# First mixture of a three-stage kernel: up products 512 columns wide, a result room for each kind of tile, four PSUM banks for transposes

## The chip, the cores and the metric

The kernel runs on one core of a Trainium2 chip. The metric is the device time of one execution in microseconds (us); three executions are timed and their median counts. The profile is one more execution, taken by the hardware profiler.

The engines are named as in the profile: PE is the matrix engine (PEld its weight loads, which overlap the products), DVE the vector engine, ACT the scalar engine, POOL the GpSimd engine, and SP the engine that issues most of the DMA transfers.

## The reference: attention, then two mixtures of experts

The rows of an attention output (4 batches of 576 tokens, 8 heads of 64) become x, 2304 rows of 512. The first mixture sends each row that passes a skip test to one of 8 experts, the second sends every row through all of 4 experts. The change is in the first:

```python
    do_compute = skip_score > 0
    xc = x[do_compute]
    e_idx = np.argmax(xc @ w_gate, axis=1)
    for e in range(E):                              # E = 8
        mask = e_idx == e
        h = np.maximum(xc[mask] @ w1[e], 0.0)       # w1[e] is 512 x 1024: the up product
        y[mask] = gate_w[mask, None] * (h @ w2[e])  # w2[e] is 1024 x 512: the down product
    out[do_compute] = xc + y
```

How many rows an expert gets is known only when the kernel runs.

## The kernel before

The program has three stages. Attention ends at about 230 us of the span; it leaves x in a DRAM buffer `XN`, and the rows that an expert will work on, each with its row number and gate weight behind it, in a DRAM buffer `XS` that has one region for each expert. The first mixture (`m1`) runs from about 235 to 410 us, and the second (`m2`) from there to the end.

`m1` goes through the experts in order. An expert's rows come in tiles of 128. Every expert has a **first tile** (the call of `m1_tile` with `y="y"`). Whether it has **further tiles** is tested on the chip by a branch on the count of rows (`more`, line 803, nested up to six deep, a loop behind it for the rest). The program holds the code of all of them; a tile that isn't needed is jumped over.

All products are made of three, to keep single precision with a fast data type: a tensor is cut into a high part and a low part (`xh`, `xl`), and high by high, high by low and low by high are added up in one PSUM bank. What `m1_tile` does for a tile of 128 rows:

- The up product, in two halves (`hf`) of 512 of the 1024 columns. Each half is one PSUM bank `hp`, filled as two quarters of 256 columns, each quarter by 12 products of 128x256 (line 710): four slices of the 512 deep sum by three. ACT takes the finished half out as `h`, with the ReLU (line 714).
- `h` is transposed on PE by four 128x128 products into a bank `tp` (`turned`, line 692), and cut into parts from there: ACT writes the high part `hi` (line 684), DVE the low part `lo` (line 685). The first half is transposed after the first quarter of the second half; the second half after the first four products of the down product (`n == self.YN`).
- `mid` transposes the rows of the next tile (`xg`, or `xi` for a further tile) in the same way, just before the down product or within it.
- The down product, 24 products of 128x512 into one bank `yp` (line 729).
- `m1_out`: DVE computes `ys` from `yp` and the rows (line 737), and POOL scatters it to `XN` by row number, with an indirect DMA (line 738). For a further tile this comes right behind the tile. For the first tile it is put off until the expert's further tiles are done (`out()` at the end of the loop over experts), so DVE does it as the next expert begins.

The `tp` tiles share a pool of two PSUM banks in turn (`ps_t`), so the third transposition of a tile goes into the bank of the first, and needs that bank read out by ACT and DVE. The `ys` tiles share two rooms in turn, in the order of the program text, in which the jumped-over tiles count.

Around the products, the weights are loaded by SP in tiles `r` of 512 KB (line 653; eight for an expert: four of `w1`, four of `w2`) and cut into a high part by ACT (line 661, `w1h`, `w2h`) and a low part by DVE (line 662, `w1l`, `w2l`). `sp` places these cuts by hand in the order of the first tile: two of this expert's `w2` tiles at its start, two more after the first half of the up product, and the next expert's four `w1` tiles after `n == 4` of the down product. On ACT and DVE the work stands in one queue in that order. In the trace experts 0 to 3 start at 237.4, 252.5, 266.3 and 280.5 us (expert 3 has one further tile, at 294.8), expert 4 at 309.8 with three further tiles, and experts 5 to 7 at 365.1, 383.3 and 397.1: 8 first tiles and 4 further ones.

Of the kernel before, what the change touches and what calls it, by code (L numbers as in the profile page):

```python
# [6 lines left out]
F32 = mybir.dt.float32  # L7
# [4 lines left out]
AF = mybir.ActivationFunctionType  # L12
ALU = mybir.AluOpType
AX = mybir.AxisListType
PSUM = bass.MemoryType.PSUM
# [37 lines left out]
class Kernel:  # L53
# [9 lines left out]
    XP = 2  # L63
    XB = 4
    YL = 5, 0
    YB = 2
    YN = 4
    LF = 99
    OT = 1
# [578 lines left out]
    def w_raw(self, w, i, e, c, pool=None):  # L648

        cols = slice(c * 256, (c + 1) * 256)  # L650
        r = pool.tile([128, 1024], F32, tag="raw", name=f"r{i + 1}") if pool else self.raw(1024, f"r{i + 1}")
        r = r.rearrange("p (k f) -> p k f", k=2 if i else 4)
        self.nc.sync.dma_start(r, (w[e, cols, :] if i else w[e, :, cols]).rearrange("(k p) f -> p k f", p=128))
        return r

    def w_split(self, pool, slot, i, raw, engines):

        hi, lo = (pool.tile([128, 1024], F32R, tag=f"w{x}{slot}", name=f"w{i + 1}{x}").rearrange(
            "p (k f) -> p k f", k=2 if i else 4) for x in "hl")
        h, l = engines  # L660
        (h.copy if h is self.nc.scalar else h.tensor_copy)(hi, raw)
        l.tensor_tensor(lo, raw, hi.bitcast(F32), ALU.subtract)
        return hi, lo
# [34 lines left out]
    def m1_tile(self, x, ws, sp=lambda n: None, mid=lambda: None, y="yi", late=0):  # L698

        nc, wk = self.nc, self.wk  # L700
        xg, xh, xl = x
        hs, hT = [], []
        sp(2)
        for hf in range(2):
            hp = self.ps_h.tile([128, 2, 256], F32, tag="h", name="hp")
            for c in range(2):
                w1h, w1l = ws[2 * hf + c]
                for i, (x, wx, k) in enumerate([(xh, wx, k) for k in range(4) for wx in (w1h, w1l)]
                                               + [(xl, w1h, k) for k in range(4)]):
                    nc.tensor.matmul(hp[:, c], lhsT=x[:, k], rhs=wx[:, k], start=(i == 0), stop=(i == 11))  # L710
                if hf and not c:
                    hT.append(self.parts(self.turned(hs[0]), "h"))
            h = wk.tile([128, 512], F32, tag="h", name="h")
            nc.scalar.activation(h, hp.rearrange("p a b -> p (a b)"), AF.Relu)
            hs.append(h)
            if not hf:
                sp(2)
        if not late:
            r = mid()
        yp = self.ps_y.tile([128, 512], F32, tag=y, name="yp")  # L720
        n = 0
        for hf in range(2):
            for x, c in [(x, c) for c in range(4) for x in range(2)] + [(2, c) for c in range(4)]:
                if late and n == late:
                    r = mid()
                if n == self.YN:
                    hT.append(self.parts(self.turned(hs[1]), "h"))
                    sp(4)
                nc.tensor.matmul(yp, lhsT=hT[hf][x // 2][:, c], rhs=ws[4 + 2 * hf + c // 2][x % 2][:, c % 2],  # L729
                                 start=(n == 0), stop=(n == 23))  # L730
                n += 1
        return r, lambda: self.m1_out(xg, yp)

    def m1_out(self, xg, yp):
        nc = self.nc
        ys = self.wk.tile([128, 512], F32, tag="y", bufs=self.YB, name="ys")
        nc.vector.scalar_tensor_tensor(ys, yp, xg[:, DM + 1:RW], xg[:, 0:DM], ALU.mult, ALU.add)  # L737
        nc.gpsimd.indirect_dma_start(out=self.XN, out_offset=bass.IndirectOffsetOnAxis(  # L738
            ap=xg[:, DM:DM + 1].bitcast(I32), axis=0), in_=ys, in_offset=None, bounds_check=N - 1, oob_is_err=False)
# [12 lines left out]
    def sp(self, n, upto):  # L752

        nc = self.nc
        en = dict(A=nc.scalar, V=nc.vector, P=nc.gpsimd)
        for _ in range(n):
            m = self.done1
            if m >= min(upto, len(self.plan)):
                return

            j = m // 2 % 6
            self.w.append([])
            self.w[-1] += self.w_split(self.wp[0 if j < 3 else 1], f"{j}{m % 2}", self.plan[m][1], self.raw1[m],
                                       [en[c] for c in self.SPE[m % 8]])
            self.done1 += 1
            self.fetch()
# [352 lines left out]
    def build(self):  # L1119
        tc, nc = self.tc, self.nc  # L1120

        def opener(st):
            return lambda name, bufs, **kw: st.enter_context(tc.tile_pool(name=name, bufs=bufs, **kw))

        with contextlib.ExitStack() as top:
            first = contextlib.ExitStack()
            top.enter_context(tc.manual_schedule() if self.MAN else contextlib.nullcontext())
            en = opener(top)
            cp, dr = en("cp", 1), en("dr", 1, space=DRAM)
            self.XS = dr.tile([E1 * N, RW], F32, name="XS")  # L1130
            self.XN = dr.tile([N, DM], F32, name="XN")
            self.ws = opener(first)("ws", self.RB)
            with contextlib.ExitStack() as st:
                en = opener(st)
                early = contextlib.ExitStack()
                self.qk, self.ep, kp = (opener(early)(x, i, side="right") for x, i in (("qk", 2), ("ep", self.EB), ("kp", 1)))
                ac = en("ac", 1)
                self.consts(cp, ac)
                self.attention_consts(ac, kp)
                self.xp = en("xp", 2)  # L1140
                self.hl, self.et, self.sm, self.sm2 = en("hl", self.HB), en("et", self.TB), en("sm", 4), en("sm2", 2)
                self.ps_s = en("ps_s", self.SB, space=PSUM)
                self.ps_t = en("ps_t", 2 if self.OT else 1, space=PSUM)
                self.ps_o = self.ps_t if self.OT else en("ps_o", 1, space=PSUM)

                def scored():

                    early.close()
                    self.ws3 = [opener(top)("wd", self.R3[0], side="right")]
                    self.wp = [opener(first)("wa", 1, side="right")]  # L1150
                    self.room += self.R3[0]

                self.attention(scored)
            with contextlib.ExitStack() as st:
                en = opener(st)
                self.wp.append(en("wb", 1))
                self.ws3.append(en("we", self.R3[1]))
                self.room += self.R3[1]
                self.wk, self.wx = en("wk", 2), en("wx", 2)
                self.ps_h, self.ps_t, self.ps_y = (en(x, i, space=PSUM) for x, i in (("ps_h", 2), ("ps_t", 2), ("ps_y", 1)))  # L1160
                raws = self.m1()
            first.close()
            en = opener(top)
            self.su, self.wu, self.wk2, self.xp = en("su", 2), en("wu", 2), en("wk2", 1), en("x2", 1)
            self.ps_u, self.ps_y = en("ps_u", self.PU, space=PSUM), en("ps_y2", 8 - self.PU, space=PSUM)
            self.m2(raws)
# [52 lines left out]
```

## Time and profile before

| | |
|---|---|
| Median of three executions | 1197.8 us (1197.21 to 1198.63) |
| The profiled execution | 1193.83 us, its span 1192.2 us |
| PE busy in the span | 1108.0 us, 93% |
| DVE, POOL, ACT busy | 767.6, 577.6, 505.9 us (64%, 48%, 42%) |
| First mixture, 235.5 to 409.7 us | 174.2 us, PE busy 160.3, DVE 102.8, ACT 92.4 |
| Mean granted clock of PE | 0.966 over the span, 0.98 in the first mixture |

The span runs from the first to the last instruction; the execution's own time is 1.6 us longer. PE counts as busy while a product is in it, and products overlap, so that a busy PE may still be slower than it could be. The granted clock is 1.00 at 2.4 GHz and 0.50 at 1.2 GHz.

### The profile page before, as it was taken

How to read it: one execution, taken by the hardware profiler on the slowest of the kernel's cores; microseconds unless marked ns; L12 is line 12 of the kernel's file. 1: busy time of each engine (PE TensorE's matmuls, PEld its weight loads, DVE VectorE, ACT ScalarE, POOL GpSimd, SP SyncE). 2: the span in 40 equal slices, each digit the busy share in tenths (PEclk: the TensorE clock that was granted, in tenths of full speed). 3: DMA queues.
4: the chain of work that ended last, by engine and by line, in shares of the span. 5: the costliest groups of instructions: out<-in, count | busy, mean ns of one | idle time of the engine just before them, and what ended most of it. 6: DMA issues, size and time to landing. Idle time of an engine off the chain costs nothing.

```text
span 1192.2 us, 19617 instructions
## 1 busy us (share of the span) xinstructions
PE 1108.0 (93%) x7485; PEld 973.3 (82%) x7485; DVE 767.6 (64%) x1227; ACT 505.9 (42%) x827; POOL 577.6 (48%) x579
## 2 busy tenths in 40 slices
PE   5889888699898779999999999999999999999998
PEld 4778887588797668988898998889888888888887
DVE  6767676578525676666666666666866667666665
ACT  5887785376425553332323233322533333333331
POOL 5968775101111065445454444545666555555551
PEclk8998899599999989999999999999999999999999
DMA  5998849499824331111111111111322111111101
GB/s 188 206 204 194 184 111 227 152 316 368 266 91 155 102 133 54 36 36 36 54 36 44 45 37 36 36 54 36 124 72 70 53 54 48 59 36 57 50 1 70
DMA packets 127248, 123.07 MB, mean 103 GB/s; under 512 B 63341, under 2 KB 96109, under 8 KB 127120
## 3 DMA queue, kind: packets, MB, share of 16 engines
q1 hardware_dynamic: 124400, 116.82, 33.8%
q0 software_dynamic: 2720, 4.64, 1.1%
q8 instruction: 69, 1.13, 0.4%
q14 instruction: 59, 0.48, 0.1%
HBM read 91.83 MB, written 19.43 MB: 93 GB/s over the span
## 4 chain that ended last, share of the span: by engine, by line
PE 62%; DVE 3%; POOL 1%; ACT 1%; DMA 0%; issue 0%; SPq 0%; POOLq 0%; ACTq 0%
PE yp L669 11%; PE yp L670 11%; PE yp L668 11%; PE hp L669 9%; PE hp L670 9%; PE hp L668 9%; DVE xsl L872 1%; PE hp L710 1%; PE yp L729 0%; DVE acc L1002 0%; DMA x<-XN 0%; PE tp L854 0%; DVE C L940 0%; POOL C L940 0%; POOL p L940 0%
## 5 line engine op out<-in xcount | busy, mean ns | idle before, releaser
L1002 DVE SCALAR_TENSOR_TENSOR acc<-yp,p,acc 128x512 f32<-128x512 f32 x270 | 199.1, 746 | 108.7 <-PE yp L670 108.6
L947 ACT ACTIVATE hh<-C 128x512 fp32r<-128x512 f32 (+2 forms) x98 | 81.7, 834 | 369.3 <-DVE C L940 328.8
L668 PE MATMUL yp<-vh,hh 128*128 128x512 f32 x576 | 226.6, 393 | 5.1 <-ACT hh L947 4.8
L669 PE MATMUL yp<-vl,hh 128*128 128x512 f32 x576 | 227.2, 394 | 1.0 <-POOL vl L917 1.0
L670 PE MATMUL yp<-vh,hl 128*128 128x512 f32 x576 | 226.4, 393 | 0.3 <-DVE hl L948 0.3
L948 DVE SCALAR_TENSOR_TENSOR hl<-C,hh 128x512 fp32r<-128x512 f32 (+2 forms) x98 | 93.2, 951 | 98.6 <-ACT hh L947 98.6
L940 POOL TENSOR_TENSOR p<-C,p 128x256 f32<-128x256 f32 (+2 forms) x49 | 50.4, 1029 | 199.4 <-ACT p L937 199.4
L670 PEld LDWEIGHTS yp<-vh,hl 128*128 128x128 f32 x576 | 108.7, 189 | 24.9 <-DVE hl L948 1.6
L668 PEld LDWEIGHTS yp<-vh,hh 128*128 128x128 f32 x576 | 109.0, 189 | 23.6 <-ACT hh L947 5.7
L669 PEld LDWEIGHTS yp<-vl,hh 128*128 128x128 f32 x576 | 109.0, 189 | 18.8 <-POOL vl L917 1.8
L917 POOL TENSOR_TENSOR vl<-r,vh 128x512 fp32r<-128x512 f32 x64 | 83.1, 1310 | 79.3 <-ACT vh L914 79.3
L940 DVE TENSOR_TENSOR C<-hp,p 128x256 f32<-128x256 f32 (+2 forms) x147 | 80.0, 544 | 35.6 <-PE hp L670 13.9
L669 PE MATMUL hp<-xsl,th 128*128 128x256 f32 (+2 forms) x294 | 97.9, 333 | 1.5 <-DVE xsl L872 1.5
L668 PE MATMUL hp<-xsh,th 128*128 128x256 f32 (+2 forms) x294 | 97.8, 333 | 0.0
L670 PE MATMUL hp<-xsh,tl 128*128 128x256 f32 (+2 forms) x294 | 97.8, 332 | 0.0
L738 POOL DMA_INDIRECT XN<-ys,xg x10 | 14.7, 1469 | 139.5 <-DVE ys L737 91.2
L302 ACT ACTIVATE E<-s,m 128x320 f32<-128x320 f32 (+4 forms) x160 | 75.9, 532 | 10.6 <-DVE m L295 9.2
L335 POOL TENSOR_TENSOR HL<-E,HL 128x1152 bf16<-128x1152 f32 (+2 forms) x37 | 63.7, 1737 | 21.9 <-ACT HL L334 14.6
L295 DVE TENSOR_REDUCE m<-s 128x1 f32<-128x576 f32 (+3 forms) x80 | 64.9, 819 | 14.1 <-PE s L286 12.6
L940 POOL TENSOR_TENSOR C<-C 128x256 f32<-128x256 f32 (+2 forms) x49 | 52.5, 1070 | 36.1 <-ACT C L937 34.8
L668 PE MATMUL hp<-xdh,dh 128*128 128x256 f32 (+2 forms) x196 | 65.1, 332 | 1.2 <-ACT xdh L861 1.2
L669 PE MATMUL hp<-xdl,dh 128*128 128x256 f32 (+2 forms) x196 | 65.2, 333 | 0.3 <-DVE xdl L862 0.3
(215 smaller groups left out, 2866.6 us busy)
## 6 DMA issues: line engine op xcount, KB each, us to landing
r<-in_w_dram SPq DMA_DIRECT2D x128, 512.0 KB, 5.8
XN<-x SPq DMA_DIRECT2D x18, 256.0 KB, 3.8
vr<-in_v_dram SPq DMA_DIRECT2D x7, 640.0 KB
xg<-XS SPq DMA_DIRECT2D x16, 257.0 KB, 5.7
out_dram<-acc SPq DMA_DIRECT2D x16, 256.0 KB, 2.0
qr<-in_q_dram SPq DMA_DIRECT2D x7, 576.0 KB, 7.4
kr<-in_k_dram SPq DMA_DIRECT2D x7, 576.0 KB, 6.4
x<-XN SPq DMA_DIRECT2D x12, 256.0 KB, 4.0
```

Source lines behind the costliest of these rows:

```text
L295: nc.vector.tensor_reduce(mo, mi, axis=ax, op=ALU.max, negate=True)
L302: nc.scalar.activation(e, views[j], AF.Exp, bias=m[:R, c:c + 1])
L335: (nc.vector if item[:2] in self.HV else nc.gpsimd).tensor_tensor(HL[:R, w:2 * w].bitcast(BF16), Et[:R, 0:w], HL[:R, 0:w], ALU.subtract)
L668: nc.tensor.matmul(out, lhsT=ah, rhs=bh, start=start, stop=False)
L669: nc.tensor.matmul(out, lhsT=ah, rhs=bl, start=False, stop=False)
L670: nc.tensor.matmul(out, lhsT=al, rhs=bh, start=False, stop=stop)
L738: nc.gpsimd.indirect_dma_start(out=self.XN, out_offset=bass.IndirectOffsetOnAxis(ap=xg[:, DM:DM + 1].bitcast(I32), axis=0), in_=ys, in_off ...
L917: nc.gpsimd.tensor_tensor(vl[:, f], r2[:, f], vh[:, f].bitcast(F32), ALU.subtract)
L940: add = lambda e, o, x, y: e.tensor_tensor(o, x, y, ALU.add)
L947: nc.scalar.activation(hh, C[:, i:i + 2], AF.Relu)
L948: V.scalar_tensor_tensor(hl, C[:, i:i + 2], 0.0, hh.bitcast(F32), ALU.max, ALU.subtract)
L1002: nc.vector.scalar_tensor_tensor(a, yp, self.p[:, n, e:e + 1], a, ALU.mult, ALU.add)
```

## The change

The four `w1` tiles of an expert are cut another way: 256 rows by 512 columns each, where they were 512 rows by 256 columns. A half of the up product is then filled by 12 products of 128x512 in place of 24 of 128x256: six from the upper 256 rows of `w1` and six from the lower ones, added up in the one bank. The `ys` of the first tiles get a room of their own and those of the further tiles another (one buffer each, where both shared two). The pool of the transposes has four PSUM banks.

```diff
--- before.py
+++ after.py
@@ -63,7 +63,6 @@
     XP = 2
     XB = 4
     YL = 5, 0
-    YB = 2
     YN = 4
     LF = 99
     OT = 1
@@ -649,14 +648,18 @@
 
         cols = slice(c * 256, (c + 1) * 256)
         r = pool.tile([128, 1024], F32, tag="raw", name=f"r{i + 1}") if pool else self.raw(1024, f"r{i + 1}")
-        r = r.rearrange("p (k f) -> p k f", k=2 if i else 4)
-        self.nc.sync.dma_start(r, (w[e, cols, :] if i else w[e, :, cols]).rearrange("(k p) f -> p k f", p=128))
+        if w is self.w11:
+            src = w[e, (c % 2) * 256:(c % 2) * 256 + 256, (c // 2) * 512:(c // 2) * 512 + 512]
+        else:
+            src = w[e, cols, :] if i else w[e, :, cols]
+        r = r.rearrange("p (k f) -> p k f", k=4 if w is self.w21 else 2)
+        self.nc.sync.dma_start(r, src.rearrange("(k p) f -> p k f", p=128))
         return r
 
     def w_split(self, pool, slot, i, raw, engines):
 
         hi, lo = (pool.tile([128, 1024], F32R, tag=f"w{x}{slot}", name=f"w{i + 1}{x}").rearrange(
-            "p (k f) -> p k f", k=2 if i else 4) for x in "hl")
+            "p (k f) -> p k f", k=2) for x in "hl")
         h, l = engines
         (h.copy if h is self.nc.scalar else h.tensor_copy)(hi, raw)
         l.tensor_tensor(lo, raw, hi.bitcast(F32), ALU.subtract)
@@ -702,16 +705,16 @@
         hs, hT = [], []
         sp(2)
         for hf in range(2):
-            hp = self.ps_h.tile([128, 2, 256], F32, tag="h", name="hp")
+            hp = self.ps_h.tile([128, 512], F32, tag="h", name="hp")
             for c in range(2):
                 w1h, w1l = ws[2 * hf + c]
-                for i, (x, wx, k) in enumerate([(xh, wx, k) for k in range(4) for wx in (w1h, w1l)]
-                                               + [(xl, w1h, k) for k in range(4)]):
-                    nc.tensor.matmul(hp[:, c], lhsT=x[:, k], rhs=wx[:, k], start=(i == 0), stop=(i == 11))
+                for i, (x, wx, k) in enumerate([(xh, wx, k) for k in range(2) for wx in (w1h, w1l)]
+                                               + [(xl, w1h, k) for k in range(2)]):
+                    nc.tensor.matmul(hp, lhsT=x[:, 2 * c + k], rhs=wx[:, k], start=(c + i == 0), stop=(c == 1 and i == 5))
                 if hf and not c:
                     hT.append(self.parts(self.turned(hs[0]), "h"))
             h = wk.tile([128, 512], F32, tag="h", name="h")
-            nc.scalar.activation(h, hp.rearrange("p a b -> p (a b)"), AF.Relu)
+            nc.scalar.activation(h, hp, AF.Relu)
             hs.append(h)
             if not hf:
                 sp(2)
@@ -729,11 +732,11 @@
                 nc.tensor.matmul(yp, lhsT=hT[hf][x // 2][:, c], rhs=ws[4 + 2 * hf + c // 2][x % 2][:, c % 2],
                                  start=(n == 0), stop=(n == 23))
                 n += 1
-        return r, lambda: self.m1_out(xg, yp)
-
-    def m1_out(self, xg, yp):
-        nc = self.nc
-        ys = self.wk.tile([128, 512], F32, tag="y", bufs=self.YB, name="ys")
+        return r, lambda: self.m1_out(xg, yp, y)
+
+    def m1_out(self, xg, yp, y):
+        nc = self.nc
+        ys = self.wk.tile([128, 512], F32, tag="s" + y, bufs=1, name="ys")
         nc.vector.scalar_tensor_tensor(ys, yp, xg[:, DM + 1:RW], xg[:, 0:DM], ALU.mult, ALU.add)
         nc.gpsimd.indirect_dma_start(out=self.XN, out_offset=bass.IndirectOffsetOnAxis(
             ap=xg[:, DM:DM + 1].bitcast(I32), axis=0), in_=ys, in_offset=None, bounds_check=N - 1, oob_is_err=False)
@@ -1157,7 +1160,7 @@
                 self.ws3.append(en("we", self.R3[1]))
                 self.room += self.R3[1]
                 self.wk, self.wx = en("wk", 2), en("wx", 2)
-                self.ps_h, self.ps_t, self.ps_y = (en(x, i, space=PSUM) for x, i in (("ps_h", 2), ("ps_t", 2), ("ps_y", 1)))
+                self.ps_h, self.ps_t, self.ps_y = (en(x, i, space=PSUM) for x, i in (("ps_h", 2), ("ps_t", 4), ("ps_y", 1)))
                 raws = self.m1()
             first.close()
             en = opener(top)
```

How this moves instructions, at three places. On PE, in the first tile of expert 0, the first quarter of the second half of the up product, before:

```order
L710 MATMUL hp<-w1h,hi 128x256
L710 MATMUL hp<-w1l,hi 128x256
L710 MATMUL hp<-w1h,hi 128x256
L710 MATMUL hp<-w1l,hi 128x256
L710 MATMUL hp<-w1h,hi 128x256
L710 MATMUL hp<-w1l,hi 128x256
L710 MATMUL hp<-w1h,hi 128x256
L710 MATMUL hp<-w1l,hi 128x256
L710 MATMUL hp<-w1h,lo 128x256 x4
```

and with the change (`hi` and `lo` are the parts of the tile's rows, `w1h` and `w1l` those of the weights):

```order
L713 MATMUL hp<-w1h,hi 128x512
L713 MATMUL hp<-w1l,hi 128x512
L713 MATMUL hp<-w1h,hi 128x512
L713 MATMUL hp<-w1l,hi 128x512
L713 MATMUL hp<-w1h,lo 128x512 x2
```

Twelve products became six of twice the width, and the low part of the rows is used from the fifth product on instead of the ninth. On PE again, right behind that place's other quarter, from the transposition of the next expert's rows to that of the second half of `h`, before (in brackets what an instruction waits for):

```order
L692 MATMUL tp<-ident,xg 128x128 [waits DMAHW5_49,PE_49]
L692 MATMUL tp<-ident,xg 128x128 x3
L729 MATMUL yp<-w2h,hi 128x512 [waits Activation_49]
L729 MATMUL yp<-w2l,hi 128x512 [waits DVE_49]
L729 MATMUL yp<-w2h,hi 128x512
L729 MATMUL yp<-w2l,hi 128x512
L692 MATMUL tp<-ident,h 128x128 [waits DVE_49,Activation_49]
L692 MATMUL tp<-ident,h 128x128 x3
```

and with the change:

```order
L695 MATMUL tp<-ident,xg 128x128 [waits DMAHW5_49]
L695 MATMUL tp<-ident,xg 128x128 x3
L732 MATMUL yp<-w2h,hi 128x512 [waits Activation_49]
L732 MATMUL yp<-w2l,hi 128x512 [waits DVE_49]
L732 MATMUL yp<-w2h,hi 128x512
L732 MATMUL yp<-w2l,hi 128x512
L695 MATMUL tp<-ident,h 128x128 [waits Activation_49]
L695 MATMUL tp<-ident,h 128x128 x3
```

The order stands; the second transposition of `h` no longer waits for DVE. On DVE, at the end of expert 3, the `ys` of its first tile, behind the joins of the branches and ahead of the low parts of expert 4's `w2`, before (DMASW are the semaphores of POOL's transfers):

```order
L803 UNCONDITIONAL_BRANCH [waits DVE_49,DVE_sequencer_49] x6
L737 SCALAR_TENSOR_TENSOR ys<-yp,xg 128x512 [waits DMASW3_49,DMASW2_49,DMASW6_49,DMASW1_49,DMASW7_49,DVE_49,PE_49]
L788 REGISTER_ALU
L1215 BRANCH_PREFETCH_HINT
L662 TENSOR_TENSOR w2l<-r_6778,w2h 128x1024 [waits DMAHW1_49,Activation_49]
```

and with the change:

```order
L806 UNCONDITIONAL_BRANCH [waits DVE_49,DVE_sequencer_49] x6
L740 SCALAR_TENSOR_TENSOR ys<-yp,xg 128x512 [waits DMASW4_49,DVE_49,PE_49]
L791 REGISTER_ALU
L1218 BRANCH_PREFETCH_HINT
L665 TENSOR_TENSOR w2l<-r_6382,w2h 128x1024 [waits DMAHW1_49,Activation_49]
```

It waits for one of POOL's transfers in place of five. On ACT, POOL and SP no instruction moves or changes its waits; the transfers of `w1` on SP have runs of 2 KB in place of 1 KB.

## Rows read from the trace of the kernel before

**Rows 1.** The page's head and its first part: busy time, share, instructions.

```profile
span 1192.2 us, 19617 instructions
PE 1108.0 (93%) x7485; PEld 973.3 (82%) x7485; DVE 767.6 (64%) x1227; ACT 505.9 (42%) x827; POOL 577.6 (48%) x579
```

**Rows 2.** Windows, the first mixture: from:to, length, engines' busy time, PE clock, DMA.

```profile
235.50:409.70 174.20, 160.32 (x1016) 140.55 (x1016) 102.81 (x111) 92.38 (x122) 17.81 (x15) 0.98 0.66 222
```

**Rows 3.** Waits from 232 to 412 us: total, times, longest, in us.

```profile
PE hp L710 <- PEq L803: 5.3, 6, 1.9
PE tp L692 <- DVE lo L685: 4.7, 2, 3.0
...
PEld tp L692 <- ACT hi L684: 2.5, 5, 0.5
```

**Rows 4.** Timeline of PE, up and down products: start, length, instruction.

```profile
253.52 0.64 PE L710 MATMUL hp<-w1h,lo 128*128 128x256 f32 x4
...
256.40 0.64 PE L710 MATMUL hp<-w1h,lo 128*128 128x256 f32 x4
...
261.79 1.09 PE L729 MATMUL yp<-w2h,lo 128*128 128x512 f32 x4
...
264.58 1.10 PE L729 MATMUL yp<-w2h,lo 128*128 128x512 f32 x4
...
275.60 1.08 PE L729 MATMUL yp<-w2h,lo 128*128 128x512 f32 x4
...
278.34 1.07 PE L729 MATMUL yp<-w2h,lo 128*128 128x512 f32 x4
```

**Rows 5.** Timeline, first tile of expert 1: PE and DVE around its third transposition.

```profile
259.55 1.28 DVE L685 TENSOR_TENSOR lo<-tp,hi 128x512 fp32r<-128x512 f32 x2
...
259.89 0.40 PE L729 MATMUL yp<-w2l,hi 128*128 128x512 f32 x1
260.38 0.63 PE L692 MATMUL tp<-ident,h 128*128 128x128 f32 x4
```

**Rows 6.** Timeline of PE: third transpositions of experts 4 and 5, starts of 2 and 6.

```profile
266.32 0.36 PE L710 MATMUL hp<-w1h,hi 128*128 128x256 f32 x1 [0.64 <-PEq L803]
...
319.32 0.63 PE L692 MATMUL tp<-ident,h 128*128 128x128 f32 x4 [1.72 <-DVE lo L685]
...
375.89 0.63 PE L692 MATMUL tp<-ident,h 128*128 128x128 f32 x4 [2.98 <-DVE lo L685]
...
383.31 0.36 PE L710 MATMUL hp<-w1h,hi 128*128 128x256 f32 x1 [0.63 <-PEq L803]
```

**Rows 7.** Timeline of DVE at the start of experts 4 and 5.

```profile
313.29 0.75 DVE L737 SCALAR_TENSOR_TENSOR ys<-yp,xg 128x512 f32<-128x512 f32 x1 [4.55 <-DMA XS<-x,sl]
313.95 4.62 DVE L662 TENSOR_TENSOR w2l<-r,w2h 128x1024 fp32r<-128x1024 f32 x4
318.49 1.28 DVE L685 TENSOR_TENSOR lo<-tp,hi 128x512 fp32r<-128x512 f32 x2
...
369.85 0.75 DVE L737 SCALAR_TENSOR_TENSOR ys<-yp,xg 128x512 f32<-128x512 f32 x1 [4.83 <-DMA XN<-ys,xi]
```

**Rows 8.** Timeline of ACT at the start of expert 4.

```profile
309.03 2.00 ACT L661 CAST w2h<-r 128x1024 fp32r<-128x1024 f32 x2 [4.84 <-PEq L803]
...
313.51 1.99 ACT L661 CAST w2h<-r 128x1024 fp32r<-128x1024 f32 x2
```

**Rows 9.** Windows, one microsecond of expert 5's down product (columns as in Rows 2).

```profile
377.00:378.00 1.00, 1.00 (x3) 0.73 (x3) 0.69 (x1) 1.00 (x2) 0.00 (x0) 0.50 1.09 382
```

**Rows 10.** Expert 4's first two further results, and landing times of all scatters.

```profile
339.96 1.00 POOL L738 DMA_INDIRECT XN<-ys,xg  x1 [23.35 <-DVE ys L737]
...
351.59 0.75 DVE L737 SCALAR_TENSOR_TENSOR ys<-yp,xi 128x512 f32<-128x512 f32 x1 [3.32 <-PE yp L729]
...
DMA to landing us min/median/max: 4.2/7.1/7.8
```

**Rows 11.** Timeline of SP: issues of one expert's eight weight tiles.

```profile
275.34 10.38 SPq L653 DMA_DIRECT2D r<-in_w_dram  x8
```

## The prediction

> **What bounds the kernel now.** I read the page's first part, then the stage that the change touches, then the waits in that stage, and last the timelines of single tiles. PE is busy for 1108.0 us of a span of 1192.2 [rows 1], so a gain has to come out of PE's own stream or out of the gaps in it. The first mixture is 174.2 us long, with PE busy for 160.3, DVE for 102.8 and ACT for 92.4 [rows 2]: PE sets its length, and about 14 us of PE's time there are gaps. Of these 5.3 us are joins of branches, six times, and 4.7 us are two stalls of a transposition behind DVE's `lo`; besides, the weight loads of five transpositions waited for 0.5 us each [rows 3]. The transposition in question is always the third of a first tile, the one that goes into the bank of the first. I take the change apart by these rows. A tile that gets shorter on PE makes the stage shorter, since the next tile starts when PE is through; the second mixture starts from the end of the first and moves forward as a whole.
>
> **Wider up products.** Expert 1's up product shows one 256-wide product in (256.40 - 253.52) / 24 = 120.0 ns, and the down product, with 512 columns, the same weight-load size and the same roles of the operands, (264.58 - 261.79) / 12 = 232.5 ns [rows 4]. Two narrow ones cost 240.0 ns, a wide one 232.5: 7.5 ns for each of 24 pairs in a tile, 0.18 us a tile, and in 12 tiles **2.2 us**. No row shows the up product itself at 512. Bounds: nothing, if a wide product there costs what two halves cost; and with expert 2's faster down product, (278.34 - 275.60) / 12 = 228.3 ns [rows 4], 11.7 ns a pair, 3.4 us. I take 2.2, from the tile where both durations stand side by side.
>
> The Trainium skill, in "TensorE: Matmul & The Clock Gate", section "Back-to-back issue gap", puts a product at full clock at its columns by 2.4 GHz plus about 2.5 ns. By that a pair would save only 2.5 ns and the term would be an estimated 0.7 us, for 288 pairs. The trace differs: 120.0 and 232.5 ns stand there against 109 and 216 by that rule.
>
> The low part of the rows is now needed at the fifth product, not at the ninth, but after the same time, 4 x 232.5 = 930 ns against 8 x 120 = 960, so DVE has 30 ns less for it. I cost this at nothing. The numbers of cuts on ACT and DVE and their sizes don't change.
>
> **The transfers of w1.** The same bytes come in runs of 2 KB, as those of `w2` do already. I cost this at nothing: SP issues an expert's eight tiles within 10.38 us [rows 11], a one-tile expert lasts 13.8 us, and thirteen rooms are filled ahead. That cover would be gone if eight tiles took more than 13.4 us; each microsecond beyond would be paid in each of four one-tile experts.
>
> **Four banks for the transposes.** In expert 1 the third transposition begins 0.49 us after the last product ahead of it, where 0.23 is the pace; DVE's two `lo` had begun at 259.55 and the first was through some 0.1 to 0.2 us before it [rows 5]. With a bank of its own it needs only `h`. That is 0.26 us in five first tiles, which the five waits of the weight loads count [rows 3]: **1.3 us**. What comes next is the ninth product, which needs that `lo`: it is 1.41 us behind the transposition (260.38 to 261.79) [rows 4, 5], so the `lo` has more than a microsecond to spare and nothing takes the wait's place. Bounds: nothing and 1.3.
>
> **Own rooms for the results.** At the start of experts 4 and 5, those behind an expert with further tiles, DVE stood idle for 4.55 and 4.83 us before the first tile's `ys` [rows 7]. What it waited for is a transfer of POOL; the names given there are an earlier scatter and the previous `ys`. The order shows the wait for five of POOL's semaphores; with the change it is for one, that of the previous first tile's scatter, issued a whole expert earlier. Behind the waiting `ys` stood four low parts of `w2` (4.62 us) and the `lo` of `h` (from 318.49) [rows 7], and for that `lo` PE waited: 1.72 us in expert 4, 2.98 in expert 5 [rows 6].
>
> What is late next when the `ys` goes at about 309: ACT cuts the first two `w2` tiles at 309.03 to 311.03 and the others at 313.51 to 315.5 [rows 8]. DVE's last two low parts then follow ACT, done near 316.8 (314.55 plus twice 1.155), and the `lo` at 317.5, against 319.1 now. PE would reach the third transposition at 317.6 (319.32 - 1.72) and the ninth product at 319.0. So both stalls go, and with the banks they would go even if only one of the two things worked in expert 4: **4.7 us**. Bounds: 3.0 (below, in the second rival) and 4.7.
>
> After expert 5's stall PE's granted clock falls to 0.50 [rows 9], which is 1.2 GHz: from the transposition to the next expert takes 383.31 - 375.89 = 7.42 us there and 266.32 - 260.38 = 5.94 in expert 1 [rows 5, 6]. The idle 1.72 us of expert 4 brought no such fall. Without the stall, 7.42 - 5.94 = **1.5 us** come back. Bounds: nothing, if another gap falls there, and 1.5.
>
> **The sum.** 2.2 + 1.3 + 4.7 + 1.5 = 9.7 us. The profiled execution had 1193.83 us (1.6 around its span), so it becomes 1184.1, with a span of 1182.5. The median of the runs is 1197.8, 4.0 above that execution, and becomes **1188.1**. What stays open on both sides are the joins: six cost 5.3 us, the shortest 0.63 and the longest 1.9 [rows 3, 6]. PE's program is shorter now, and a jump passes less of it; I put this at nothing, with 1.2 us either way.
>
> **The rivals.** *The width buys nothing.* A wide product costs two narrow ones, because the streaming itself is the limit; the trace speaks against it with 7.5 ns a pair, though never in the up product. 9.7 - 2.2 = 7.5 us, 1190.3. By the formula of the Trainium skill above it would be an estimated 1189.6.
>
> *The room isn't what DVE waited for.* The `ys` might still be late behind another of POOL's transfers. Then the `lo` comes at 319.1 in expert 4 and near 375.8 in expert 5 (369.85 plus 0.66, 4.62 and 0.64), and PE, no longer held at the transposition, is held at the ninth product, due at 319.0 and at 375.89 - 2.98 + 1.41 = 374.3: 0.1 and 1.5 us in place of 1.7 and 3.0. The gain of this term is 3.0 to 3.1 instead of 4.7; in all 8.1 us, 1189.7. Against it speaks the order, which leaves one old transfer.
>
> *DVE becomes the bound of the one-tile experts.* It does eight low parts (9.24 us), three `lo` (1.92) and a `ys` (0.75) there, 11.9 us [rows 7] of now 13.8, and 13.4 with the change. If all that DVE stands idle now, 1.9 us, were links that can't shrink, the 0.44 us of four such experts would be lost: 1.8 us, 1189.9. Against it: DVE waits there for ACT, which waits for PE.
>
> *The joins take it back.* If each of the six cost as much as the longest, 6 x 1.85 - 5.3 = 5.8 us are lost: 1193.9. Nothing in the diff touches the branches.
>
> *The single room stalls DVE: slower.* Further tiles' results now share one room, so the second of an expert waits for the scatter of the first to land. In expert 4 that scatter is issued at 339.96 and the next `ys` starts at 351.59, 11.6 us later; the longest landing is 7.8 us [rows 10]. It stalls only from 11.6 us on, and two tiles can be hit (the second and third further one). To lose the 9.7 us and 0.2% of the time (2.4 us), each would have to lose 6 us: landings near 17.7 us, more than twice the longest seen. The time would be 1200.2.
>
> **How the numbers follow.** Two kernels that differ by under 0.2%, about 2.4 us, can't be told apart by measuring this one. Chances: my sum 0.68, the width for nothing 0.10, the room not the cause 0.07, DVE as the bound 0.05, the joins 0.03, the single room or a wait of its kind 0.07, of which I put 0.03 on slower and 0.04 on no change. That gives 0.93 for faster. The range: the sum's bounds are 3.4 in place of 2.2 for the width and 1.2 for the joins, to 1185.7, and 1.2 for runs that differ (the three lie 1.4 us apart, and the profiled one 4.0 below): 1184.5. Upward it takes in the width, the room and DVE as single cases and the two largest together (2.2 + 1.8 = 4.0), to 1192.1; with the runs 1192.5. Joins and single room stay out, one in ten.
>
> **What would show it.** In the profile after: the stage some 9.7 us shorter; the up products as 288 of 128x512 at about 232 ns start to start; no wait of a transposition for DVE's `lo`, and about 0.23 us from the fourth down product to the third transposition; no idle DVE ahead of the first tile's `ys` in experts 4 and 5; a clock of 1.00 in all of expert 5. The prediction is wrong if DVE still stands idle for 4 us there, if a new wait stands ahead of the ninth down product, if the up product's pace is 240 ns, or if the joins grow.

## The result, and the profile after

The changed kernel takes 1176.74 us (four executions, 1175.39 to 1179.44) against 1197.51 for the one before beside it (four, 1191.24 to 1198.63): a ratio of 0.9841 [0.9815, 0.9866] (the 95% interval in brackets), some 19 us. The forecast was 1188.1 with a range of 1184.5 to 1192.5; the kernel is faster than the range allows.

The profiled execution is one of 1179.44 us. First the page's head and busy times, which answer to [rows 1]:

```profile
span 1177.8 us, 19008 instructions
PE 1101.1 (93%) x7197; PEld 954.4 (81%) x7197; DVE 767.4 (65%) x1227; ACT 506.4 (43%) x827; POOL 577.2 (49%) x579
```

The 288 products that were merged are gone from PE's count, and PE is busy 6.9 us less. The first mixture, between the same events as in [rows 2] (first transposition of rows to the start of the last `ys`), in windows:

```profile
232.50:395.90 163.40, 156.07 (x728) 123.94 (x728) 103.16 (x111) 92.42 (x122) 16.94 (x15) 0.98 0.68 237
```

It is 10.8 us shorter than the 174.2 of [rows 2], where 9.7 were forecast. The spans differ by 14.4. Of the other 3.6 us, 2.9 lie in attention, which the change doesn't reach: its last product (`tot`) starts at 226.71 us, and at 229.65 in the profile before. The second mixture differs by 0.5.

The waits of the stage, to be read beside [rows 3] (total, times, longest, in us):

```profile
PE hp L713 <- PEq L806: 3.9, 6, 1.0
PE hp L713 <- ACTq L806: 1.0, 1, 1.0
...
DVE ys L740 <- DVEq L806: 3.1, 7, 0.6
```

PE no longer waits for a `lo` of DVE at any transposition. Six joins (what PE stands idle behind the branches, ahead of the next expert's first product) went from 5.3 to 3.9 us, where I had forecast no change. There is a seventh, ahead of expert 3, which the view puts down to ACT: 1.0 us here, and in the kernel before

```profile
PE hp L710 <- ACTq L803: 1.1, 1, 1.1
```

which [rows 3] don't have. All seven went from 6.4 to 4.9 us. PE's timeline, in the columns of [rows 4, 6]:

```profile
250.78 0.62 PE L713 MATMUL hp<-w1h,lo 128*128 128x512 f32 x2
...
253.50 0.62 PE L713 MATMUL hp<-w1h,lo 128*128 128x512 f32 x2
...
256.94 0.40 PE L732 MATMUL yp<-w2l,hi 128*128 128x512 f32 x1
257.17 0.60 PE L695 MATMUL tp<-ident,h 128*128 128x128 f32 x4
...
264.00 0.63 PE L713 MATMUL hp<-w1h,lo 128*128 128x512 f32 x2
...
266.79 0.63 PE L713 MATMUL hp<-w1h,lo 128*128 128x512 f32 x2
...
304.56 0.49 PE L713 MATMUL hp<-w1h,hi 128*128 128x512 f32 x1 [1.02 <-PEq L806]
...
311.95 0.60 PE L695 MATMUL tp<-ident,h 128*128 128x128 f32 x4
...
364.41 0.60 PE L695 MATMUL tp<-ident,h 128*128 128x128 f32 x4
```

In expert 1 the wide up product goes at (253.50 - 250.78) / 12 = 226.7 ns, in expert 2 at (266.79 - 264.00) / 12 = 232.5. The third transposition follows the fourth down product by 0.23 us (257.17 - 256.94), and in experts 4 and 5 (311.95, 364.41) it carries no wait any more. From expert 5's to the next tile PE's clock (the third figure from the right) is full, where [rows 9] had half clock:

```profile
364.00:369.70 5.70, 5.57 (x27) 4.29 (x25) 4.95 (x7) 4.77 (x6) 0.00 (x0) 1.00 0.82 270
```

On DVE, the `ys` ahead of which it stood for 4.55 and 4.83 us in [rows 7], and between them the second further `ys` of expert 4:

```profile
304.92 0.75 DVE L740 SCALAR_TENSOR_TENSOR ys<-yp,xg 128x512 f32<-128x512 f32 x1 [0.59 <-DVEq L806]
...
343.76 0.75 DVE L740 SCALAR_TENSOR_TENSOR ys<-yp,xi 128x512 f32<-128x512 f32 x1 [3.32 <-PE yp L732]
...
357.53 0.75 DVE L740 SCALAR_TENSOR_TENSOR ys<-yp,xg 128x512 f32<-128x512 f32 x1 [0.58 <-DVEq L806]
```

Only the join itself is left ahead of the first and the last. The one between waits for its product, for 3.32 us as in [rows 10], and not for the single room. Every mechanism that the forecast named is there, then; but the gain is 9 us larger than forecast in the timed runs.

### The profile page after: what moved, and what is told of

It reads as the page before. It is cut to its first block, busy times and chain, and to the rows that moved or that the text cites. A ratio compares the mean times of both kernels' runs of the same rounds, so it can differ in the third digit from the quotient of the medians.

```text
span 1177.8 us, 19008 instructions
## 1 busy us (share of the span) xinstructions
PE 1101.1 (93%) x7197; PEld 954.4 (81%) x7197; DVE 767.4 (65%) x1227; ACT 506.4 (43%) x827; POOL 577.2 (49%) x579
## 4 chain that ended last, share of the span: by engine, by line
PE 62%; DVE 2%; POOL 1%; ACT 1%; issue 0%; DMA 0%; SPq 0%; POOLq 0%; ACTq 0%
PE yp L672 11%; PE yp L671 11%; PE yp L673 11%; PE hp L672 10%; PE hp L673 9%; PE hp L671 9%; DVE xsl L875 1%; PE yp L732 0%; PE hp L713 0%; PE tp L857 0%; DVE acc L1005 0%; POOL vl L920 0%; DVE C L943 0%; POOL C L943 0%; DVE xdl L865 0%
```

## The experiments

The first theory (A) was that each part does what its term says and the rest of the timed gain is how executions differ. Its rival (B) was that the longer runs of the `w1` transfers shorten something outside the stage, attention above all. Times are medians, ratios are against the kernel before on the same chip, and a gain in us is what the ratio takes off that kernel's median.

**The parts alone.** Only the hunks of the change on `w1` and the up product:

```diff
-            src = w[e, :, cols]
+            src = w[e, (c % 2) * 256:(c % 2) * 256 + 256, (c // 2) * 512:(c // 2) * 512 + 512]
...
-                    nc.tensor.matmul(hp[:, c], lhsT=x[:, k], rhs=wx[:, k], start=(i == 0), stop=(i == 11))
+                    nc.tensor.matmul(hp, lhsT=x[:, 2 * c + k], rhs=wx[:, k], start=(c + i == 0), stop=(c == 1 and i == 5))
```

> Only the w1 tiles of 256 by 512 and the 512-wide up products; two shared result rooms and two transpose banks as before. Theory A (all of the gain is made in the first mixture, the rest of the measured 20 us is the clock falling differently from execution to execution): the stage shorter by 2 to 3 us (up products at 227 to 233 ns against 240 for a pair), the stalls of 1.7 and 3.0 us behind the low part still there, time 2 to 3 us below the kernel before. Theory B (the 2 KB runs of w1 also relieve the transfers at the end of attention): a further 6 to 9 us come out of the stretch from 190 us to the first transposition of the mixture, time 8 to 12 us below.

1190.61 us, ratio 0.9962 [0.9938, 0.9985]. The stage is 171.3 us, 2.9 less than in [rows 2]; 1.7 of this lie in the seven joins (4.7 us in place of 6.4), so that the 2.9 don't price the width. Both stalls are still there, as its PE timeline shows:

```profile
320.45 0.63 PE L696 MATMUL tp<-ident,h 128*128 128x128 f32 x4 [2.53 <-DVE lo L689]
...
376.99 0.63 PE L696 MATMUL tp<-ident,h 128*128 128x128 f32 x4 [2.56 <-DVE lo L689]
```

Expert 4's is 0.8 us longer than in [rows 6], expert 5's 0.4 shorter, and this time the clock fell behind expert 4's (7.95 us from there to the next tile) and not behind expert 5's (5.72).

The transfers alone, with products of 256 columns out of the new tiles:

```diff
-                    nc.tensor.matmul(hp[:, c], lhsT=x[:, k], rhs=wx[:, k], start=(i == 0), stop=(i == 11))
+                    nc.tensor.matmul(hp[:, cs], lhsT=x[:, k], rhs=ws[2 * hf + k // 2][j][:, k % 2, cs], start=(i == 0), stop=(i == 11))
```

> Only the w1 tiles of 256 by 512, read by 256-wide products in the old order; rooms and banks as before. Theory A: same time as before within 1 us, in the stage and in whole. Theory B: 6 to 9 us below, all of it ahead of the first mixture's first transposition.

1196.08 us, ratio 0.9995 [0.9973, 1.0017]: runs of 2 KB in place of 1 KB buy nothing that the timing shows, 3.2 us at most by the interval. B had asked for 6 to 9 us, and attention's last product came at 235.8 us here, later than in either profile above, so B falls.

Only the rooms:

```diff
-        ys = self.wk.tile([128, 512], F32, tag="y", bufs=self.YB, name="ys")
+        ys = self.wk.tile([128, 512], F32, tag="s" + y, bufs=1, name="ys")
```

> Only the own result rooms. Theory A: no idle vector engine ahead of the first tile's result in experts 4 and 5, both stalls gone (at most 0.3 us left, since the bank is still shared), no fall of the clock in expert 5: the stage 6 to 6.5 us shorter, time the same amount below. Theory B says the same of this kernel. If the room is not the cause, the idle 4.5 us stay and nothing is gained.

1187.98 us, ratio 0.9943 [0.9916, 0.9969]. Stage 167.9 us. Its waits:

```profile
PE hp L709 <- PEq L802: 5.2, 6, 1.7
...
PEld tp L691 <- ACT hi L683: 3.5, 7, 0.5
```

Both stalls are gone with the rooms alone, and DVE stands for 0.59 and 0.57 us ahead of the `ys` in experts 4 and 5, while the half-microsecond waits that the banks remove are still there, seven now, since experts 4 and 5 have one too. So the room is what DVE waited for, and the rival that denied it falls.

Only the banks:

```diff
-                self.ps_h, self.ps_t, self.ps_y = (en(x, i, space=PSUM) for x, i in (("ps_h", 2), ("ps_t", 2), ("ps_y", 1)))
+                self.ps_h, self.ps_t, self.ps_y = (en(x, i, space=PSUM) for x, i in (("ps_h", 2), ("ps_t", 4), ("ps_y", 1)))
```

> Only four transpose banks. Theory A: the vector engine still idles 4.5 and 4.8 us ahead of the result, the third transposition waits for nothing, and the matrix engine waits instead at the ninth down product, 0.1 us in expert 4 and 1.5 us in expert 5; with 1.3 us from the five other first tiles and 1.5 us if the clock then holds, 4 to 6 us below. Theory B says the same.

1187.56 us, ratio 0.994 [0.9913, 0.9967]. Stage 171.1 us. From PE's timeline:

```profile
303.05 0.55 PE L710 MATMUL hp<-w1h,hi 128*128 128x256 f32 x1 [2.71 <-PEq L803]
...
368.83 1.19 PE L729 MATMUL yp<-w2h,lo 128*128 128x512 f32 x4 [1.68 <-DVE lo L685]
```

With the `ys` still late (DVE idle for 5.54 us ahead of it in expert 4 and 5.17 in expert 5), expert 5 is held at the ninth down product for 1.68 us; the second rival had put 1.5 there. In expert 4 PE doesn't wait there. The join ahead of expert 4 took 2.71 us, longer than any of [rows 3], and the clock was low behind it. One microsecond of that, in windows:

```profile
304.00:305.00 1.00, 1.00 (x7) 1.00 (x6) 0.00 (x0) 0.27 (x1) 0.00 (x0) 0.50 0.05 12
```

**The whole again, without the width, and before again.** The changed kernel unchanged; rooms and banks together; the kernel before unchanged:

> The changed kernel once more, with many runs of both kernels on one chip. Theory A (the stage alone): its stage 10.8 to 11.2 us shorter than before, as in its first profile, and the time 11 to 13 us below the median of the many runs of before, not 19 to 21. A rival, theory C (something outside the first mixture gains too): still 17 us or more below.

1181.94 us, ratio 0.9889 [0.9861, 0.9917], 13.3 us off 1194.1, where theory C had asked for 17 or more. Its stage is 163.8 us; its attention ends sooner still:

```profile
L491 PE MATMUL tot<-hist,ones x1: 190/190/190, 222.2 to 222.2; 128*128 128x9 bf16 x1
```

> Own rooms and four banks, narrow up products from the old w1 tiles. Theory A: both stalls gone for the rooms' sake and the five bank waits for the banks' sake: stage 7.5 to 8 us shorter (rooms alone 6.3, banks' five waits 1.3), time the same amount below. The parts don't add up: rooms alone and banks alone each remove most of the same two stalls. If they added up, 9.4 us in the stage and 14 in time.

1185.43 us, ratio 0.9926 [0.9897, 0.9955]. Stage 168.5: no stall, but the join ahead of expert 4 took 2.18 us, PE's clock fell to 0.50 behind it, and the tile took 15.50 in place of 14.34 in the kernel with rooms alone. That is why the expected 7.5 to 8 us of the stage are 5.7 here.

> The kernel before as an experiment: ratio 1 within 0.2%, a stage of 174 us with the two stalls, and another length of attention than in the first profile (229.6 us to its last product), by several us either way, since nothing in the first mixture can reach it. Theory C has no say here.

1195.3 us, ratio 1.0002 [0.998, 1.0024]; as it should be for the same program. The profile was the surprise: the same program has a stage of 179.5 us here, 5.3 longer than in [rows 2]. In windows, and below it the joins from its waits, all seven:

```profile
232.20:411.70 179.50, 162.12 (x1016) 142.21 (x1016) 103.03 (x110) 92.48 (x122) 17.84 (x15) 0.97 0.64 216
...
PE hp L710 <- PEq L803: 7.4, 7, 2.0
```

PE's timeline, where it is longer (the join ahead of expert 4 is shorter, 0.90 us in place of 1.85):

```profile
264.30 0.36 PE L710 MATMUL hp<-w1h,hi 128*128 128x256 f32 x1 [1.63 <-PEq L803]
...
279.37 0.36 PE L710 MATMUL hp<-w1h,hi 128*128 128x256 f32 x1 [1.99 <-PEq L803]
...
284.91 0.28 PE L710 MATMUL hp<-w1h,hi 128*128 128x256 f32 x1 [1.70 <-issue]
...
319.28 0.72 PE L692 MATMUL tp<-ident,h 128*128 128x128 f32 x4 [2.21 <-DVE lo L685]
...
378.04 1.09 PE L692 MATMUL tp<-ident,h 128*128 128x128 f32 x4 [3.14 <-DVE lo L685]
```

and a window behind the stall of expert 4, at half clock:

```profile
320.00:321.00 1.00, 1.00 (x4) 0.81 (x3) 0.29 (x1) 0.92 (x2) 0.00 (x0) 0.50 1.02 335
```

In the first profile the stall was shorter [rows 6], and no fall followed it:

```profile
320.00:321.00 1.00, 1.00 (x6) 0.79 (x5) 0.35 (x1) 0.97 (x2) 0.00 (x0) 1.00 1.09 335
```

From that transposition to the next tile it took 7.97 us, and 6.42 in the first profile.

**Is it the code that a join passes?** The joins are the term that varied without a cause. If a join costs by the jumped-over code (D1), a program that nests four further tiles in place of six must have shorter ones. Both kernels were built so, the executed work the same:

```diff
-    CM = 6
+    CM = 4
```

> The kernel before with the nesting of further tiles cut from six to four deep, so that two tile bodies of eight per expert are not in the program (this data never uses them): 10285 rows on the matrix engine in place of 11245, about what the wide products save (10221). Nothing that runs is changed. Theory D1 (a join costs by the code that is passed over): the six joins cost 3.7 to 4.5 us in place of 5.3 to 7.4, time 1 to 2 us below. Theory D2 (the joins got shorter with the wide products because the engine then eats instructions at half the rate around them): joins of 5 to 7 us as before, time the same.

1194.92 us, ratio 0.9974 [0.9947, 1.0]. The joins:

```profile
PE hp L710 <- PEq L803: 6.2, 7, 1.9
```

All seven are 6.2 us, against 6.4 and 7.4 in the two profiles before. Without expert 3's, the one that [rows 3] don't count, they are 4.4 against 5.3 and 5.4, which is in D1's range; but the lengths behind this (0.64 us ahead of expert 2, 0.90 ahead of expert 4) stand in one or the other of those profiles, too, so this profile can't tell D1 from chance. The stalls are 2.87 and 3.13, with a fall behind the first (7.95 to the next tile).

> The changed kernel with the nesting cut to four. D1: joins of 3 us or less in place of 3.9 to 4.5, stage about 162.5 us. D2: joins and stage as in the changed kernel, 163.2 to 163.8.

1183.64 us, ratio 0.9883 [0.9849, 0.9917]; the joins:

```profile
PE hp L713 <- PEq L806: 4.9, 7, 1.4
```

All seven are 4.9 us, against 4.9 and 5.5 with the full nest; without expert 3's they are 4.4, where D1 asked for 3 or less. So D1 isn't shown, and fails here. For the kernel before it isn't excluded: the interval of the time would allow its 1 to 2 us, too.

**The changed kernel a third time, and without the width.** The second has everything of the change except the 512 columns (the product line of the transfers' experiment above):

> The changed kernel a third time: a stage of 163 to 164 us again, with no stall and no half clock inside it from the second tile on, whatever the length of attention in that execution; time 13 to 15 us below before. If its stage, too, varies by 5 us from execution to execution as that of the kernel before did (174.2 and 179.5), then the variation isn't made by the stalls that the change removes.

1182.1 us, ratio 0.9881 [0.9849, 0.9913], 14.3 us. The stage, in windows:

```profile
231.30:394.50 163.20, 155.41 (x728) 123.47 (x728) 102.93 (x111) 92.37 (x122) 17.86 (x15) 0.99 0.68 237
```

> The changed kernel with the up products 256 wide, from the same w1 tiles of 256 by 512: width alone is undone. If the width is worth the 2.2 us of the prediction, the stage is 165.5 to 166 us; with the pace that the changed kernel's trace shows (227 ns against 239 for a pair) and with joins back at 5.2 to 5.7 us, 167.5 to 168.5 us, as with rooms and banks on the old tiles. Time 3 to 5 us above the changed kernel.

1183.39 us, ratio 0.9888 [0.9853, 0.9924]. The stage in the same columns:

```profile
231.60:397.40 165.80, 157.99 (x1016) 140.47 (x1016) 102.57 (x110) 92.41 (x122) 17.21 (x15) 0.98 0.66 233
```

Against 163.2 to 163.8 with the wide products, the width is worth 2.0 to 2.6 us. The joins are 5.6 us, all seven, no longer than in the changed kernel's third profile; so the wide products (D2) aren't needed for shorter joins. (The intervals of the two timed ratios overlap: a couple of microseconds can't be told apart by timing here.)

**Before, a third look.** Is the stage of 174.2 us or that of 179.5 the usual one?

> One more look at the kernel before, for its stalls. The first profile, from which the prediction was worked out, showed 1.7 us in expert 4 with no fall of the clock behind it, and a stage of 174.2 us; the two other executions of this kernel had 2.2 and 2.9 us, a fall to half clock behind each, and 179.5 and 178.8. If the first was the mild case, this one shows a stall of over 2 us in expert 4, a time from it to the next tile of 7.9 us in place of 6.4, and a stage of 176 to 180 us. If the first was the usual case, 1.7 us, 6.4 and 174 to 175.

1194.04 us (one execution; the one beside it 1189.41). The stage runs from 230.42 to 410.35, 179.9 us, the long case that I had put down:

```profile
230.40:410.40 180.00, 164.29 (x1016) 144.14 (x1016) 102.90 (x111) 92.40 (x122) 17.80 (x15) 0.95 0.64 215
```

PE's timeline:

```profile
278.11 0.40 PE L710 MATMUL hp<-w1h,hi 128*128 128x256 f32 x1 [1.99 <-PEq L803]
...
317.92 0.63 PE L692 MATMUL tp<-ident,h 128*128 128x128 f32 x4 [2.21 <-DVE lo L685]
...
325.88 0.39 PE L710 MATMUL hp<-w1h,xih 128*128 128x256 f32 x1 [0.68 <-ACT xih L684]
```

and windows behind the join and behind the stall:

```profile
279.00:280.00 1.00, 1.00 (x6) 1.00 (x6) 1.00 (x2) 0.81 (x1) 0.56 (x1) 0.50 1.10 355
...
320.00:321.00 1.00, 1.00 (x4) 0.81 (x3) 0.81 (x1) 1.00 (x2) 0.00 (x0) 0.50 1.08 384
```

Again 7.96 us from the stall to the next tile. And here the join of 1.99 us into expert 3 was followed by half clock, which it wasn't in the second profile of this kernel.

**The tiles side by side.** From the first up product of one tile to that of the next on PE's timeline, in us, joins included. The column behind them is the sum over eleven tiles, from expert 0's first up product to expert 7's, and the last one the seven joins in it.

| kernel | expert 1 | 2 | 3 | 3, further | 4 | 5 | sum | joins |
|---|---|---|---|---|---|---|---|---|
| before, first profile | 13.82 | 14.19 | 14.29 | 15.00 | 15.94 | 18.19 | 159.7 | 6.4 |
| before, second | 14.81 | 15.07 | 15.84 | 14.07 | 17.97 | 18.85 | 165.0 | 7.4 |
| before, third | 14.74 | 15.07 | 15.76 | 14.05 | 17.96 | 18.88 | 165.5 | 7.3 |
| before, nest of four | 13.82 | 14.90 | 15.71 | 14.04 | 18.62 | 18.74 | 164.3 | 6.2 |
| transfers alone | 13.82 | 14.15 | 14.31 | 14.03 | 17.93 | 18.21 | 160.6 | 5.6 |
| width and transfers | 13.62 | 14.04 | 14.20 | 13.84 | 18.06 | 15.91 | 156.9 | 4.7 |
| rooms alone | 13.82 | 14.12 | 14.27 | 14.91 | 14.34 | 13.72 | 153.4 | 6.2 |
| banks alone | 13.53 | 13.83 | 14.01 | 15.88 | 15.37 | 15.63 | 156.6 | 7.5 |
| rooms and banks | 13.59 | 13.85 | 14.00 | 15.36 | 15.50 | 13.43 | 154.1 | 6.7 |
| all but the width | 13.53 | 13.85 | 14.00 | 14.31 | 14.00 | 13.43 | 151.4 | 5.6 |
| changed, first | 13.21 | 13.70 | 13.85 | 14.05 | 13.76 | 13.15 | 148.9 | 4.9 |
| changed, second | 13.27 | 13.69 | 13.85 | 14.53 | 13.78 | 13.16 | 149.4 | 5.5 |
| changed, third | 13.23 | 13.70 | 13.85 | 14.53 | 13.77 | 13.16 | 148.8 | 5.6 |
| changed, nest of four | 13.29 | 13.16 | 13.88 | 14.45 | 13.77 | 13.17 | 148.8 | 4.9 |

The changed kernel repeats within 0.6 us. The one before has tiles that come out at either of two lengths: expert 4 at 15.94 or near 18, expert 3 at 14.3 or 15.8, the join ahead of expert 2 takes 0.64 or 1.6 us, that ahead of expert 3 1.1 or 2.0.

The joins part by the `w1` tiles. The seven profiles with the old ones have 6.2 to 7.5 us, and a longest join of 1.75 to 2.71; the seven with the new ones have 4.7 to 5.6, and a longest join of 1.01 to 1.51. Two of these have narrow products (5.6). And a join is long only where transfers run. Ahead of experts 5 and 7, with a DMA share of at most 0.06 in the microsecond around its start, all 28 joins took 0.53 to 0.89 us; the twelve of 1.4 us or more, all ahead of experts 2 to 4, had shares of 0.28 to 1.07. The join ahead of expert 4 in the first and the second profile before (1.85 and 0.90 us; the share is the last figure but one):

```profile
307.35:308.35 1.00, 0.60 (x3) 0.17 (x1) 0.36 (x1) 0.00 (x0) 0.00 (x0) 1.00 0.61 190
...
307.78:308.78 1.00, 0.60 (x3) 0.17 (x1) 0.36 (x1) 0.27 (x1) 0.00 (x0) 1.00 0.00 0
```

Transfers don't always make a join long: ahead of experts 1 and 6 it took at most 0.76 us with shares up to 1.11. That they are the cause isn't shown.

## Why the prediction was wrong

**The width** was sized rightly: 2.2 us forecast, 2.0 to 2.6 measured, of which 0.1 to 0.7 are shorter joins. The rest is 7 to 9 ns for each of the 264 pairs in the table's eleven tiles. The Trainium skill ("TensorE: Matmul & The Clock Gate", section "Back-to-back issue gap") gives an isolated product at full clock about 2.5 ns beside its columns. By that the term would be an estimated 0.7 us; the runs decide against that here.

**The transfers of w1** at nothing: measured as 0.9995, with up to 3.2 us open by the interval. The shorter joins that go with the new tiles (with narrow products 5.6 us in place of 6.2 to 7.5) would, if the tiles cause them, be a gain that this term left out. The earlier need for the `lo` of the rows cost nothing that shows.

**The banks** did what was said, 0.23 us from the fourth down product to the third transposition. The term of 1.3 us is right, too: with rooms and banks, the tiles of experts 1, 2, 3, 5 and 6 are 0.23 to 0.29 us shorter than with the rooms alone, 1.35 in all. That they also take the transposition's part of the stalls was in the text; alone they leave the 1.68 us at the ninth product. Rooms and banks overlap on the stalls, and so their gains alone (6.8 and 7.2 us timed) can't be added.

**The rooms** removed both stalls and the fall of the clock, as said. The step that failed is the size of this term and of the fall behind it, 4.7 + 1.5 = 6.2 us, with "1.72 in expert 4, 2.98 in expert 5", and "The idle 1.72 us of expert 4 brought no such fall". All of it is true of one execution, and that was a mild one. In the two later profiles of the same program the stalls are 2.21 and 3.13 or 3.14 us; half clock follows expert 4's, too, and costs 1.5 more (7.97 and 7.96 us to the next tile, 6.42 in the first); behind expert 5's it costs 1.3 and 1.5. Stalls and falls come to 8.2 and 8.3 us there. A further 1.5 goes to an issue gap or to half clock in expert 3 (15.84 and 15.76 in place of 14.29), which the changed kernel doesn't have. With the sums of the table the change gains 165.0 - 149.4 = 15.6 to 165.5 - 148.8 = 16.7 us against those two executions, and 10.3 to 10.9 against the one that I worked from.

**The joins** at nothing, with 1.2 us either way, was the second mis-sized term: all seven take 4.9 to 5.6 us in the changed kernel against 6.4 to 7.4 before, some 0.9 to 1.5 less than in the first profile and 1.8 to 2.4 less than in the later ones. I counted six of them, and priced a rival only for a loss there.

**The allowance for runs** of 1.2 us rested on three executions that lay 1.4 us apart by luck; at the upper end the sum has only 0.4 for them (1192.1 to 1192.5). In the later comparisons the kernel before ran from 1186.41 to 1205.56. Part of that is attention, whose last product came between 222.2 and 235.8 us in the profiles. The mean stage of three profiles each is 177.9 us before and 163.5 with the change, 14.4 less; the later comparisons give 13.3 and 14.3 us. The first one's 19, with 16.0 at the low end of its interval, is more than the stage accounts for on average, and that rest stays open. The forecast's 9.7 is below all three intervals.

So the mechanisms held, and the rivals of the forecast fell. The one-tile experts got shorter (expert 1: 13.82 us before, at most 13.27 with the change), so DVE didn't become their bound. Open: what makes a join take 0.64 or 2.0 us in the same place of the same program (the amount of code jumped over isn't shown to, by two runs; the long ones had transfers in flight), why it is shorter with the new `w1` tiles, and why attention's length moves. That the changed kernel is steadier because it has no stall and no long join is what the table suggests; no run isolates it.

## What to carry to other kernels

One profile gives one execution: take a second before a stall, a join or a clock fall is priced, and put the longer case into the range where a gap that long was followed by half clock anywhere in the trace. A change that removes stalls removes what they bring in longer executions too; a gain worked out from a mild one comes out too small, as here. Parts that remove the same stall must be costed together, and the second place at which the late work is needed tells what is left if only one works.

## What the runs showed of the hardware

- Half clock behind a gap of PE isn't decided by the gap's length alone: none behind stalls of 1.72 and 2.56 us and joins of 1.75 and 1.85, a fall behind stalls of 2.21 (twice), 2.22, 2.53, 2.87 and 2.98 to 3.14 (five) and joins of 1.87, 2.18 and 2.71; behind the same join of 1.99 us none in one execution and a fall in another. A fall cost about 1.5 us (7.97 - 6.42 behind expert 4's stall, 15.76 - 14.29 in expert 3's first tile).
- The same join of the same program took 0.64 us in one execution and 1.63 in another, and 1.85 us elsewhere in the first where the second had 0.90. All joins of 1.4 us or more had transfers in flight around their start (a DMA share of 0.28 to 1.07), and with a share of at most 0.06 ahead of experts 5 and 7 none took more than 0.89.
- Wide up products ran at 226.7 ns in expert 1 and 232.5 in expert 2, the second the price that I had taken from [rows 4]. Against two narrow ones (240.0) that is 13.3 and 7.5 ns a pair; over all tiles 7 to 9 are left.
